# Finishing one tile ahead of the other in a layer's last down phase, and letting VectorE scale in the first K phase

## The chip, the cores and the metric

The kernel runs on one core of a Trainium2 chip. The metric is the device time of one execution in microseconds (us), lower is better. Most executions of one kernel lie within 0.2% of their median, some 2 us here.

## The reference, cut to what matters

Two identical layers act on 2048 tokens of 576 channels. Each has a linear attention and a gated unit without a nonlinearity; both layers share their weights.

```python
def _A_ref(x, wqkv, w_phi, wo):                      # 32 heads of 18
    ...
    phi_q = concatenate([softmax(pq), softmax(-pq)]) # the same for phi_k
    kv  = einsum("bhsf,bhsd->bhfd", phi_k, v)        # a sum over ALL tokens
    z   = einsum("bhsf->bhf", phi_k)
    num = einsum("bhqf,bhfd->bhqd", phi_q, kv)
    ...
def _B_ref(x, w_gate, w_up, w_down):                 # 576 -> 4608 -> 576
    return einsum("bsf,fd->bsd", einsum(x, w_gate) * einsum(x, w_up), w_down)

for layer in (1, 2):
    x = x + _A_ref(_layernorm(x), wqkv, w_phi, wo)
    x = x + _B_ref(_layernorm(x), w_gate, w_up, w_down)
```

The sum over all tokens is what makes a seam: layer 2 can attend only when the last tile of layer 1 has gone through its down projection, its normalisation and its K and V.

## The kernel before

Tokens are worked on in 16 tiles of 128, two tiles to a block, so each layer has eight blocks. A block has a gate/up phase and then a down phase. The engine programs are laid out on the host by a list scheduler: tasks yield groups of instructions, and the scheduler takes the group that it believes can start first, from the fixed durations that are written into each `Op`. What a task waits for in the schedule ("wait", "sig") is not a wait on the chip; it only fixes the order in which instructions are issued.

The down phase sums both tiles step by step (36 steps, 512 + 64 columns for each tile). The 64 column sums of both tiles share bank Z:

```python
def t_down(self, L, b, on_block_done):
    gots = yield ("acqn", ["pb"], 3)
    X, Y, Z = [g_[1] for g_ in gots]
    for f in range(NF):                              # NF = 36
        c, fi = divmod(f, CH)                        # CH = 2 steps to one load
        if fi == 0:
            yield ("wait", ("wd", L, b, c))
        ops = []
        for sl in range(2):                          # both tiles in every step
            ops.append(Op(... matmul(ps[:, X or Y, 0:512], lhsT, w[:, 0:512]) ...))
            ops.append(Op(... matmul(ps[:, Z, 64 * sl:64 * sl + 64], lhsT, w[:, 512:576]) ...))
        yield ("ops", "pe", ops)
        if fi == CH - 1:
            yield ("rel", "wd", slot)                # the ring slot is free for the next load
    yield ("go", s.t_bepi(L, b, X, Y, Z, on_block_done), 8, ...)

def t_bepi(self, L, b, X, Y, Z, on_block_done):      # one task: tile 0's adds, then tile 1's
    ...
    for sl in range(2):
        yield ("ops", "dve", [add of 512 columns, add of 64 columns])
        yield ("sig", ("x2t", L, st_))
```

The down weights come through a ring of six slots (five `wdr` and one `wdx`), one load of 288 KB for two steps; 18 loads make a phase. The scaling of the normalisation is offered to several engines; `boot` is the first K phase, `fast` the two tiles at the seam:

```python
yield ("alt", [(eng, [Op(...)...])
       for eng, dur in (("pool", (800, 200)[:2 - fast]), ("dve", (400,)))[:1 + fast]]
       + ([("act", act)] if boot else []))
```

## Time and profile before

| what | value |
|---|---|
| time | 1115.49 us, median of 3 (1114.45 to 1117.24) |
| span of the profiled execution | 1113.9 us |
| TensorE busy | 1069.7 us, 96% of the span |
| K phase, until the first gate/up weight load (on the cut told under the result) | 117.6 us |
| last down phase of layer 1 to layer 2's first gate/up | 53.3 us |
| start of the last down phase to the end | 21.9 us |

A profile is read here from coarse to fine. The busy row and the 40 slices show which engine is full and where it is not. Where it is not, a chain or a timeline shows what it waits for; in a timeline line the columns are start, duration, engine, source line, operation, output and inputs, shapes, and in brackets the idle time before and what ended it. The lines themselves are in the prediction below.

### The profile page before, as it was taken

The page shows a single profiled execution, that of the slowest core. Times are in us where ns is not written, and L with a number is a line of the kernel's source. Part 1 is how long each engine was busy: PE and PEld are TensorE (multiplying, and loading weights), DVE is VectorE, ACT ScalarE, POOL GpSimd, SP SyncE. Part 2 cuts the span into 40 slices and gives each one's busy share as a digit, 9 for nine tenths or more (in the row PEclk, how much of TensorE's full clock was granted, in tenths as well). Part 3 has the DMA queues.
Part 4 walks back from the last instruction along what each step waited for, and adds up shares of the span by engine and source line. Part 5 has one row for each costly group of instructions (what it writes and reads, how often), then busy time and mean ns, then how long its engine had stood idle before and what let it go on. Part 6 is the DMA issues. An engine that isn't in the chain of part 4 may idle for free.

```text
span 1113.9 us, 33734 instructions
## 1 busy us (share of the span) xinstructions
PE 1069.7 (96%) x15280; PEld 835.1 (75%) x15342; DVE 588.4 (53%) x1184; ACT 374.4 (34%) x862; POOL 313.3 (28%) x334
## 2 busy tenths in 40 slices
PE   5788999999999999999999899999999999999998
PEld 4565886868687786869687678696969696969685
DVE  7788744647375564646453675444535353524231
ACT  7786631414133241414232463131313030402120
POOL 4885512424152432413220252121212030300000
PEclk9899999999999999999999999999999999999999
DMA  8494227273542616371523313717272726362604
GB/s 175 114 314 157 32 47 197 47 204 47 151 97 79 158 39 186 47 204 26 152 75 98 96 24 47 214 36 215 35 215 35 205 46 191 58 180 49 179 26 139
DMA packets 185002, 129.07 MB, mean 116 GB/s; under 512 B 103322, under 2 KB 183706, under 8 KB 183706
## 3 DMA queue, kind: packets, MB, share of 16 engines
q1 hardware_dynamic: 184858, 126.91, 44.4%
q8 instruction: 120, 1.97, 0.7%
q14 instruction: 24, 0.20, 0.0%
HBM read 100.75 MB, written 2.36 MB: 93 GB/s over the span
## 4 chain that ended last, share of the span: by engine, by line
PE 83%; DVE 7%; ACT 4%; DMA 3%; POOL 2%; issue 1%; SPq 0%; DVEq 0%; POOLq 0%; ACTq 0%
PE ps L1427 47%; PE ps L1497 20%; PE ps L1001 6%; PE ps L1500 4%; PE ps L989 3%; PE ps L1288 2%; DMA wdr<-in_B_w_down_dram 1%; PE ps L1169 1%; DVE ss L1116 1%; DVE dd L1048 1%; POOL dd L1127 1%; ACT hT L1473 1%; DVE mxmn L1034 1%; DVE hT L1475 1%; DVE mxmn L1029 1%
## 5 line engine op out<-in xcount | busy, mean ns | idle before, releaser
L1427 PE MATMUL ps<-xT,Wu 64*128 64x256 bf16 x4608 | 582.2, 269 | 0.0
L1427 PE MATMUL ps<-xT,Wg 64*128 64x256 bf16 x4608 | 579.8, 269 | 0.8 <-ACT xT L971 0.8
L1427 PEld LDWEIGHTS ps<-xT,Wu 64*128 64x128 bf16 x4608 | 431.8, 94 | 22.4 <-DVE hT L1475 1.6
L1427 PEld LDWEIGHTS ps<-xT,Wg 64*128 64x128 bf16 x4608 | 427.2, 94 | 27.0 <-issue 3.3
L1473 ACT CAST hT<-ps 128x512 bf16<-128x512 f32 x288 | 168.0, 583 | 567.8 <-PE ps L1427 526.6
L1475 DVE TENSOR_TENSOR hT<-ps,hT 128x512 bf16<-128x512 f32 x288 | 196.9, 689 | 216.1 <-ACT hT L1473 215.3
L1497 PE MATMUL ps<-wdr,hT 128*128 128x512 bf16 x913 | 237.3, 380 | 0.9 <-DMA wdr<-in_B_w_down_dram 0.9
L1427 PE MATMUL ps<-xT,Wr 64*128 64x256 bf16 x1152 | 190.0, 269 | 0.0
L1500 PE MATMUL ps<-wdr,hT 128*128 128x64 bf16 x960 | 185.0, 193 | 3.1 <-DMA wdr<-in_B_w_down_dram 0.4
L1497 PEld LDWEIGHTS ps<-wdr,hT 128*128 128x128 bf16 x960 | 93.8, 98 | 110.8 <-DMA wdr<-in_B_w_down_dram 2.5
L1127 POOL TENSOR_TENSOR dd<-dd,ss 128x576 bf16<-128x576 bf16 x119 | 136.8, 1172 | 124.9 <-ACT ss L1123 121.0
L1098 POOL TENSOR_TENSOR dd<-xT,mxq 128x576 bf16<-128x576 bf16 x56 | 63.9, 1163 | 320.6 <-DVE mxq L1094 320.6
L1522 DVE TENSOR_TENSOR x_sb<-ps,x_sb 128x512 bf16<-128x512 f32 x32 | 22.0, 687 | 225.6 <-PE ps L1500 225.6
L961 POOL TENSOR_SCALAR xln<-x_sb,nmean,rstd 128x576 bf16<-128x576 bf16 x104 | 62.5, 607 | 172.9 <-ACT rstd L950 108.8
L1116 DVE TENSOR_REDUCE ss<-dd 128x64 f32<-128x1152 bf16 x61 | 82.1, 1347 | 31.6 <-ACT dd L1110 31.5
L1500 PEld LDWEIGHTS ps<-wdr,hT 128*128 128x128 bf16 x960 | 94.3, 98 | 0.0
L1427 PEld LDWEIGHTS ps<-xT,Wr 64*128 64x128 bf16 x1152 | 82.8, 94 | 5.2
L1108 ACT ACTIVATE dd<-dd 128x576 bf16<-128x576 bf16 x61 | 41.7, 684 | 47.6 <-DVE dd L1048 30.9
L1039 POOL TENSOR_TENSOR dd<-psb,mxmn 128x576 bf16<-128x576 bf16 x26 | 30.2, 1163 | 80.6 <-DVE mxmn L1029 80.6
L1497 PE MATMUL ps<-wdx,hT 128*128 128x512 bf16 x177 | 50.8, 380 | 0.0
L933 DVE BATCH_NORM_STATS2 st<-x_sb 128x6 f32<-128x288 bf16 x120 | 46.0, 446 | 2.8 <-DMA x_sb<-in_A_x_dram 2.7
L1001 PE MATMUL ps<-Wo,oT 64*128 64x288 bf16 x504 | 44.0, 283 | 0.8
(123 smaller groups left out, 968.9 us busy)
## 6 DMA issues: line engine op xcount, KB each, us to landing
wdr<-in_B_w_down_dram SPq DMA_DIRECT2D x240, 288.0 KB, 3.5
wdx<-in_B_w_down_dram SPq DMA_DIRECT2D x48, 288.0 KB, 3.4
Wg<-in_B_w_gate_dram SPq DMA_DIRECT2D x4, 1152.0 KB, 16.4
Wu<-in_B_w_up_dram SPq DMA_DIRECT2D x4, 1152.0 KB, 18.5
x_sb<-in_A_x_dram SPq DMA_DIRECT2D x8, 288.0 KB, 3.1
out_dram<-x_sb SPq DMA_DIRECT2D x16, 144.0 KB, 2.3
Wraw<-in_A_wqkv_dram SPq DMA_DIRECT2D x8, 144.0 KB, 2.8
xT<-xln SPq DMA_TRANSPOSE x58, 2.6
```

What stands on the lines that cost most here:

```text
L933: ops.append(Op(d_dve(288), (lambda e, j=j, h=h, src=src: e.bn_stats(st[:, sl[j], 6 * h:6 * h + 6], src)), reads=rd, writes=[("st", sl[j], ...
L961: em = [(lambda e, j=j, a=a, b=b, c=c: e.tensor_scalar(xln[:, sl[j], a:b], x_sb[:, ss[j], c:c + b - a], s.nmean[:, sl[j]:sl[j] + 1], rstd[ ...
L1001: out.append(Op(61, (lambda e, h=h, k=k, st=(i == 0 and k == 0), sp=(i == 1 and k == 3): e.matmul(s.ps[:, banks[h], 0:N], L[r, k, :], Wm[r ...
L1098: yield ("ops", "pool", [Op(1150, (lambda e, d=d, mb=mb: e.tensor_tensor(d, p3, mb, ALU.subtract)), reads=[("xT", st_), ("mq", mq, br)], w ...
L1108: yield ("ops", "act", [Op(590, (lambda e: e.activation(de2, de2, ACTF.Exp, scale=-1.0)), reads=s.ddk(sm, 1), writes=s.ddk(sm, 1))])
L1116: Op(1320, (lambda e: e.tensor_reduce(ss[:, sm, :].rearrange("p (b g) -> p b g", b=2), e4, AX.X, ALU.add)), reads=s.ddk(sm, 0) + s.ddk(sm, ...
L1127: yield ("alt", [(eng, [Op(dur, (lambda e, ev=ev, rb=rb: e.tensor_tensor(ev, ev, rb, ALU.mult)), reads=s.ddk(sm, br) + [("ss", sm)], write ...
L1427: out.append(Op(54.3, (lambda e, bank=bank, cs=cs, lhsT=lhsT, rhs=rhs, st=st, sp=sp: e.matmul(ps[:, bank, cs].rearrange("p (a n) -> p a n" ...
L1473: yield ("ops", "act", [Op(540, (lambda e, gb=gb, p=p: e.copy(hT[:, p, :], ps[:, gb, :])), reads=[("gu", gb)], writes=[("hT", p)] + (s.raw ...
L1475: yield ("ops", "dve", [Op(625, (lambda e, ub=ub, p=p: e.tensor_tensor(hT[:, p, :], ps[:, ub, :], hT[:, p, :], ALU.mult)), reads=[("gu", u ...
L1497: ops.append(Op(d_pe(512), (lambda e, lhsT=lhsT, bank=bank, slot=slot, fi=fi, f=f: e.matmul(ps[:, bank, 0:512], lhsT, s.wslot(slot)[:, fi, ...
L1500: ops.append(Op(d_pe(64) + 3, (lambda e, lhsT=lhsT, sl=sl, slot=slot, fi=fi, f=f: e.matmul(ps[:, Z, 64 * sl:64 * sl + 64], lhsT, s.wslot(s ...
```

## The change

The intent has two parts. In the last down phase of each layer, TensorE finishes the first tile's sums three ring slots (six steps) ahead of the second's, so that tile 0's sum can be added and normalised (layer 1) or stored (layer 2) while tile 1 is still being summed. For that the phase takes a fourth bank, so tile 0's 64 columns can be read alone. And in the first K phase VectorE joins GpSimd and ScalarE as an engine that may scale a tile. Two details apply to all sixteen down phases: in the last step the 64 column matmul is issued before the 512 column one, and the adds of the two tiles are two tasks, each of which takes its 64 columns first.

```diff
--- before.py
+++ after.py
@@ -565,6 +565,7 @@
         self.pqp = (5, 5)
         self.pqg = 12
         self.NPQ = 2
+        self.NLAST = 3
         self.pqd = 100
         self.pqn = (16, 16)
         self.qcrit = False
@@ -961,7 +962,7 @@
             em = [(lambda e, j=j, a=a, b=b, c=c: e.tensor_scalar(xln[:, sl[j], a:b], x_sb[:, ss[j], c:c + b - a], s.nmean[:, sl[j]:sl[j] + 1], rstd[:, sl[j]:sl[j] + 1],
                                                                  ALU.add, ALU.mult)) for a, b, c in ((0, 576, 0), (576, 640, 512))[:2 - fast]]
             yield ("alt", [(eng, [Op(d, em[i], reads=[("x", ss[j], 0), ("x", ss[j], 1), ("nmean", sl[j]), ("rstd", sl[j])], writes=[("xln", sl[j])]) for i, d in enumerate(dur)])
-                           for eng, dur in (("pool", (800, 200)[:2 - fast]), ("dve", (400,)))[:1 + fast]] + ([("act", act)] if boot else []))
+                           for eng, dur in (("pool", (800, 200)[:2 - fast]), ("dve", (400,) if fast else (400, 200)))[:1 + (fast or boot)]] + ([("act", act)] if boot else []))
         for j in js:
             if fast:
                 (_, bank), = yield ("acqn", ["pb"], 1)
@@ -1481,52 +1482,74 @@
 
     def t_down(self, L, b, on_block_done):
         s = self
-        ps, hT = s.ps, s.hT
-        gots = yield ("acqn", ["pb"], 3)
-        X, Y, Z = [g_[1] for g_ in gots]
-        for f in range(NF):
+        hT = s.hT
+
+        last = b == NB - 1
+        NR = NF - CH * s.NLAST * last
+        gots = yield ("acqn", ["pb"], 3 + last)
+        X, Y, Z = [g_[1] for g_ in gots][0:3]
+        ZZ = (Z, gots[3][1]) if last else (Z, Z)
+
+        def mm(f, sl):
+            c, fi = divmod(f, CH)
+            slot = s.wd_slot[(L, b, c)]
+            bank = X if sl == 0 else Y
+            z = ZZ[sl]
+            c0 = 256 * (f % 2) + 128 * sl
+            lhsT = hT[:, f // 2, c0:c0 + 128]
+            rd = [("hT", f // 2), ("wdr", slot)]
+            ops = [Op(d_pe(512), (lambda e: e.matmul(s.ps[:, bank, 0:512], lhsT, s.wslot(slot)[:, fi, 0:512], start=(f == 0), stop=(f == NF - 1))),
+                      reads=rd, writes=[("acc", bank)], excl=[("pb", bank)]),
+                   Op(d_pe(64) + 3, (lambda e: e.matmul(s.ps[:, z, 64 * sl:64 * sl + 64], lhsT, s.wslot(slot)[:, fi, 512:576],
+                                                        start=(f == 0 and (sl == 0 or last)), stop=(f == NF - 1), skip_group_check=True)),
+                      reads=rd, writes=[("acc", z)], excl=[("pb", z)])]
+            return ops[::-1] if f == NF - 1 else ops
+
+        for f in range(NR):
             c, fi = divmod(f, CH)
             if fi == 0:
                 yield ("wait", ("wd", L, b, c))
-            slot = s.wd_slot[(L, b, c)]
-            ops = []
-            for sl in range(2):
-                bank = X if sl == 0 else Y
-                c0 = 256 * (f % 2) + 128 * sl
-                lhsT = hT[:, f // 2, c0:c0 + 128]
-                ops.append(Op(d_pe(512), (lambda e, lhsT=lhsT, bank=bank, slot=slot, fi=fi, f=f: e.matmul(
-                    ps[:, bank, 0:512], lhsT, s.wslot(slot)[:, fi, 0:512], start=(f == 0), stop=(f == NF - 1))),
-                    reads=[("hT", f // 2), ("wdr", slot)], writes=[("acc", bank)], excl=[("pb", bank)]))
-                ops.append(Op(d_pe(64) + 3, (lambda e, lhsT=lhsT, sl=sl, slot=slot, fi=fi, f=f: e.matmul(
-                    ps[:, Z, 64 * sl:64 * sl + 64], lhsT, s.wslot(slot)[:, fi, 512:576],
-                    start=(f == 0 and sl == 0), stop=(f == NF - 1), skip_group_check=True)),
-                    reads=[("hT", f // 2), ("wdr", slot)], writes=[("acc", Z)], excl=[("pb", Z)]))
-            yield ("ops", "pe", ops)
+            yield ("ops", "pe", mm(f, 0) + mm(f, 1))
             if fi == CH - 1:
-                yield ("rel", "wd", slot)
+                yield ("rel", "wd", s.wd_slot[(L, b, c)])
+        for sl in range(2):
+            for f in range(NR, NF):
+                c, fi = divmod(f, CH)
+                if fi == 0:
+                    yield ("wait", ("wd", L, b, c))
+                yield ("ops", "pe", mm(f, sl))
+                if sl == 1 and fi == CH - 1:
+                    yield ("rel", "wd", s.wd_slot[(L, b, c)])
+            if sl == 0 and last:
+                for nxt, prio, name in on_block_done(L, b):
+                    yield ("go", nxt, prio, name)
+                yield ("go", s.t_bepi(L, b, 0, X, ZZ[0], True), 11, "bepi%d" % b)
         s.dn_active = False
         yield ("sig", ("dn", L, b))
-        yield ("go", s.t_bepi(L, b, X, Y, Z, on_block_done), 8, "bepi%d" % b)
-
-    def t_bepi(self, L, b, X, Y, Z, on_block_done):
-        s = self
-        ps, x_sb = s.ps, s.x_sb
-        for nxt, prio, name in on_block_done(L, b):
-            yield ("go", nxt, prio, name)
-        for sl in range(2):
-            st_ = 2 * b + sl
-            bank = X if sl == 0 else Y
-            xa = x_sb[:, st_, 0:512]
-            xb = x_sb[:, st_, 512:576]
-            yield ("ops", "dve", [
-                Op(d_dve(512), (lambda e, xa=xa, bank=bank: e.tensor_tensor(xa, ps[:, bank, 0:512], xa, ALU.add)),
-                   reads=[("acc", bank), ("x", st_, 0)], writes=[("x", st_, 0)], excl=[("pb", bank)]),
-                Op(d_dve(64), (lambda e, xb=xb, sl=sl: e.tensor_tensor(xb, ps[:, Z, 64 * sl:64 * sl + 64], xb, ALU.add)),
-                   reads=[("acc", Z), ("x", st_, 1)], writes=[("x", st_, 1)], excl=[("pb", Z)])])
-            yield ("rel", "pb", bank)
-            yield ("sig", ("x2t", L, st_))
-        yield ("rel", "pb", Z)
-        yield ("sig", ("x2", L, b))
+        if not last:
+            for nxt, prio, name in on_block_done(L, b):
+                yield ("go", nxt, prio, name)
+            yield ("go", s.t_bepi(L, b, 0, X, Z, False), 8, "bepi%d" % b)
+        yield ("go", s.t_bepi(L, b, 1, Y, ZZ[1], True), 11 if last else 8, "bepi%d" % b)
+
+    def t_bepi(self, L, b, sl, bank, z, free):
+        s = self
+        st_ = 2 * b + sl
+        if sl == 1:
+            yield ("wait", ("x2t", L, st_ - 1))
+        xa = s.x_sb[:, st_, 0:512]
+        xb = s.x_sb[:, st_, 512:576]
+        ops = [Op(d_dve(512), (lambda e: e.tensor_tensor(xa, s.ps[:, bank, 0:512], xa, ALU.add)),
+                  reads=[("acc", bank), ("x", st_, 0)], writes=[("x", st_, 0)], excl=[("pb", bank)]),
+               Op(d_dve(64), (lambda e: e.tensor_tensor(xb, s.ps[:, z, 64 * sl:64 * sl + 64], xb, ALU.add)),
+                  reads=[("acc", z), ("x", st_, 1)], writes=[("x", st_, 1)], excl=[("pb", z)])]
+        yield ("ops", "dve", ops[::-1])
+        yield ("rel", "pb", bank)
+        if free:
+            yield ("rel", "pb", z)
+        yield ("sig", ("x2t", L, st_))
+        if sl == 1:
+            yield ("sig", ("x2", L, b))
 
     def t_store(self, b):
         s = self
```

## The prediction

> **What bounds the kernel now.** I read the page first (busy shares and the 40 slices), then the chain that ended last in order of time, then the timeline and the busy table of the places that the change touches. The page says that this is a TensorE kernel with two soft spots:
>
> ```profile
> PE 1069.7 (96%) x15280; PEld 835.1 (75%) x15342; DVE 588.4 (53%) x1184; ACT 374.4 (34%) x862; POOL 313.3 (28%) x334
> ...
> PE   5788999999999999999999899999999999999998
> ```
>
> TensorE is busy in nine tenths of every slice but the first four (a slice is 27.8 us), slice 23 and the last one. The first four are the first K phase (layer 1 normalises, projects K and V and sums its state); slice 23 is the seam in which layer 1's last block has to be summed, normalised and turned into K before layer 2 can start. Between them run the sixteen gate/up and down phases, where TensorE is full: nothing that the change does can shorten those. The change removes no matmul, so only the three places where TensorE waits can pay: **the K phase, the seam, the end.** The table of these stretches (busy time of each engine):
>
> ```profile
> core 0: us, PE busy (x) PEld busy (x) DVE busy (x) ACT busy (x) POOL busy (x), PEclk, DMA share, GB/s
> 12.00:101.00 89.00, 68.24 (x562) 49.04 (x560) 78.34 (x160) 67.53 (x182) 65.38 (x65) 0.88 0.67 190
> ...
> 618.90:653.30 34.40, 28.97 (x268) 22.29 (x266) 26.60 (x59) 20.06 (x52) 9.58 (x8) 1.00 0.08 25
> ```
>
> In the K phase VectorE is the busiest engine, 78.34 of 89 us, with GpSimd at 65.38. In the seam TensorE fills itself with Q projections, but the chain through it is VectorE and ScalarE work on the last two tiles. Its start, in VectorE's timeline:
>
> ```profile
> 618.88 0.69 DVE L1522 TENSOR_TENSOR x_sb<-ps,x_sb 128x512 bf16<-128x512 f32 x1 [15.67 <-PE ps L1500]
> 619.49 0.22 DVE L1524 TENSOR_TENSOR x_sb<-ps,x_sb 128x64 bf16<-128x64 f32 x1
> 619.74 0.82 DVE L933 BATCH_NORM_STATS2 st<-x_sb 128x6 f32<-128x288 bf16 x2
> ...
> 621.40 0.43 DVE L961 TENSOR_SCALAR xln<-x_sb,nmean,rstd 128x576 bf16<-128x576 bf16 x1 [0.41 <-ACT rstd L950]
> 621.75 0.68 DVE L1522 TENSOR_TENSOR x_sb<-ps,x_sb 128x512 bf16<-128x512 f32 x1
> ```
>
> Tile 0's sum starts at 618.88, just when the down phase ends. Tile 1's sum is ready at the same moment but is taken at 621.75, after tile 0's whole normalisation. So the two tiles are ready together and are then served one after the other; an earlier tile 0 moves the queue. The end shows the same pair:
>
> ```profile
> 1109.58 0.69 DVE L1522 TENSOR_TENSOR x_sb<-ps,x_sb 128x512 bf16<-128x512 f32 x1 [16.13 <-PE ps L1500]
> 1110.19 0.21 DVE L1524 TENSOR_TENSOR x_sb<-ps,x_sb 128x64 bf16<-128x64 f32 x1
> 1110.32 0.68 DVE L1522 TENSOR_TENSOR x_sb<-ps,x_sb 128x512 bf16<-128x512 f32 x1
> 1110.43 1.09 SPq L1535 DMA_DIRECT2D out_dram<-x_sb  x2
> 1110.92 0.21 DVE L1524 TENSOR_TENSOR x_sb<-ps,x_sb 128x64 bf16<-128x64 f32 x1
> ```
>
> Two tiles' adds follow the last matmul serially, then the second store lands (2.3 us, median of the page's DMA table); the span is over at 1113.9.
>
> **What the Trainium skill says.** "PSUM — Partial Sum Buffer", section "PSUM bank collisions raise a hardware error": two engines must not be in one bank at once, so accesses are guarded by bank, not by address. That is why the change takes a fourth bank in the last phase: the 64 leftover columns of both tiles share bank Z now, and tile 0's could not be read while tile 1's are still being summed. No run here shows a collision; the kernel orders accesses by bank. "SBUF — State Buffer", section "Who interferes with whom": a VectorE instruction with two SBUF inputs, or one in a two-port mode such as tensor_scalar can enter, shuts GpSimd out for its whole length. The trace agrees as to the first kind: the GpSimd multiply that starts at 635.89, beside a VectorE multiply of 0.76 us, takes 1.73 us, where the group's mean is 1172 ns. "VectorE: DVE Perf Modes", section "The perf-mode tier table", lets tensor_scalar on bf16 run at four elements a cycle; the trace has 429 ns for 576 elements (mean of 6), which is 1.34 elements a ns, well short of that rate, so I use 429.
>
> **The change, part by part.**
>
> (1) *Order of the last down phase.* A down step is 512 + 64 columns for each tile. In the timeline one tile's pair starts every 0.245 us (1094.71, 1094.95, 1095.20). Three ring slots are 6 steps, so tile 0 runs its last 6 pairs in 6 x 0.245 = 1.47 us, then tile 1 its 6 in another 1.47 us. TensorE's total is unchanged; tile 0's sum is ready 5 to 6 pairs earlier than now, about 1.4 us, if the weights are there.
>
> (2) *Are the weights there?* Two tiles drain a slot in 0.98 us, one tile alone in 0.49. Tile 0 thus wants the next-to-last slot 0.49 us and the last slot 0.98 us earlier than today. At the seam the next-to-last slot is late already:
>
> ```profile
> 611.89 5.05 DMA wdr<-in_B_w_down_dram
> 616.94 0.05 issue
> 616.98 0.39 PE ps L1497
> ```
>
> (The chain: the load issued at 611.89 lands at 616.94; TensorE waits 0.23 us.) The same load would now be wanted at 616.75 - 0.49 = 616.26, so TensorE waits about 0.7 us instead of 0.2, and runs tile 0's last two slots from 616.98 to about 617.96. Tile 0 is ready there instead of at about 618.7: **0.7 us earlier, half of the ideal.** Tile 1 then ends 6 x 0.245 later, 619.4, against 618.9 now; but it isn't wanted before tile 0's normalisation has left VectorE. At the end of the kernel the loads took 2.9 to 4.3 us (median 3.6) and nothing waited: the last one, issued at 1103.97, should land near 1107.6, and tile 0 would want it at about 1107.9. I count no stall there.
>
> (3) *Seam.* VectorE's queue there starts 0.7 us sooner, and tile 1's add, now behind tile 0's scaling, moves with it: 618.88 to 621.75 is 2.87 us of VectorE sequence, so tile 1 would be taken at about 618.05 + 2.87 = 620.9, well after its sum is there (619.4). From 621.4 to 637.6 the chain alternates between VectorE, ScalarE, TensorE's 1.4 us projections and a GpSimd multiply, without slack that I could name, so the 0.7 us should reach the start of layer 2's gate/up at 653.29. Taking the 64 columns first (they wait for a matmul that ends before the 512 one) may add 0.1. **Seam: -0.8 us.**
>
> (4) *End.* Tile 0's two adds (0.8 us) and its store now lie under tile 1's matmuls. After the last matmul, whose end stays near 1109.8, only tile 1's 512 add (0.68) is left, so it is done at 1110.5 instead of 1111.13 (1110.92 + 0.21). **End: -0.6 us.**
>
> (5) *Scaling on VectorE in the first K phase.* Of the 16 tiles GpSimd scales 10 now (820 + 393 ns each, 1.21 us with both parts) and ScalarE 6 (866 + 245 ns, and a 0.29 us product before it, 1.40 us). VectorE would need 429 ns for 576 columns and, estimated from its small instructions (0.15 to 0.26 us for 64 columns or fewer), 0.2 for the rest: 0.63 us. What it can relieve:
>
> ```profile
> 17.84 2.60 POOL L961 TENSOR_SCALAR xln<-x_sb,nmean,rstd 128x576 bf16<-128x576 bf16 x4 [1.04 <-ACT rstd L950]
> ...
> 25.00 1.39 POOL L853 TENSOR_TENSOR BDphi<-wst,mask 128x720 bf16<-128x720 bf16 x1 [3.44 <-DMA wst<-in_A_w_phi_dram]
> ...
> 27.49 1.31 POOL L961 TENSOR_SCALAR xln<-x_sb,nmean,rstd 128x576 bf16<-128x576 bf16 x2
> ...
> 29.91 1.31 POOL L961 TENSOR_SCALAR xln<-x_sb,nmean,rstd 128x576 bf16<-128x576 bf16 x2
> ```
>
> The chain of the first 35 us runs along these GpSimd lines. The two tiles at 17.84 sit ahead of a wait for the phi weights (3.44 us), which would absorb what is saved there. The two at 27.49 and 29.91 had their rstd from ScalarE long before and only queue behind that wait; on VectorE they would be done two to three us sooner and GpSimd's multiplies, which release TensorE's sums at 32.40, would come 2.6 us sooner. Against this, VectorE is full from 10 to 32 us (10.00 of 10.00 in 20 to 30) and then idles for 1.92 us before 34.21 and 2.23 before 37.79. The schedule is laid out on the host by a greedy list scheduler that gives each tile to the engine it believes free first, with VectorE's cost weighted by 1.2; I guess that 4 to 7 tiles move, 2.5 to 4.4 us more on the busiest engine, most of it paid out of those idle stretches. From 83 to 101 us VectorE works without a gap, so what is gained early is passed on only if its backlog there also starts earlier. I choose **-1.2 us**, with a spread of some 2.5 either way, because a different order of issue reshuffles the whole phase.
>
> (6) *A fourth bank.* At the last down phase of layer 2 six banks belong to gate/up, whose first pair is free by then, and two to nobody: four are there, no wait. In layer 1 the state sums of layer 2 (from 599.70) take one bank at a time with a higher priority, so the phase may start a little later or have its order against them changed: +0.2 us, a guess within the 1.7 us that these sums take.
>
> Sum: -0.8 - 0.6 - 1.2 + 0.2 = -2.4 us, so 1115.49 - 2.4 = **1113.1 us.**
>
> **The rivals.** *The weights eat it all*: if the last two loads at the seam come later still (the largest landing time there is 5.0 us), tile 0 gains nothing and TensorE ends 1 us later, so seam and fourth bank together cost about +0.5: total near 1114.0. For it speaks the wait that is already there; against it that only one of 16 down phases matters. *VectorE becomes the bound of the K phase*: with 78 of 89 us busy, 6 tiles x 0.63 = 3.8 us more could lengthen the phase by up to that: 1117. For it the gapless stretch from 83 us on; against it some 10 us of idle VectorE earlier, where the scaling lies. *GpSimd's chain was the bound*: four tiles fewer take 4 x 1.21 = 4.8 us off it, and all of it arrives: near 1109.5. *Nothing but the end survives*, because the scheduler puts the scaling where it would have waited anyway: 1114.9.
>
> **Range and chances.** The two sure pieces are small (1.4 us together); the K phase sets the spread. I give 1109.0 to 1116.5, which covers all but the worst of the rivals. Two per cent would be 22.3 us; the whole of TensorE's idle time in the span is 1113.9 - 1069.7 = 44 us, and only some 15 us of it lie where the change acts. Chances: faster by over 2% 0.02, within 2% 0.96, slower 0.02.
>
> **What would show it.** In the changed trace: the first of the two last 512 adds should begin over 1 us before the last matmul, and the end of the last add should follow that matmul by about 0.7 us; at the seam, tile 0's add at 0.7 us before its present place relative to the start of that down phase, with a wait for a wdr load of about 0.7 us in TensorE's list; the time from tile 0's add to layer 2's first gate/up unchanged at 34.4 us; 4 to 7 tiles of scaling on VectorE before 60 us, and the first gate/up (now 117.85) starting 1.2 us sooner. I am wrong if the K phase moves by more than 3 us either way, if a new wait for a bank shows at the start of the last down phase, or if the gate/up and down phases in between change length by more than 1 us, which I take as fixed.

## The result, and the profile after

| | before | after |
|---|---|---|
| median, us | 1114.97 (1113.39 to 1117.24, 4 runs) | 1111.77 (1111.19 to 1112.81, 4 runs) |
| span of the profiled execution, us | 1113.9 | 1109.5 |

The ratio is 0.9971, with a 95% interval of 0.9951 to 0.999: 3.2 us faster. A ratio here is the mean time of one kernel's fast runs over that of the other's from the same rounds, so it is not quite the ratio of the medians. The predicted 1113.1 us is 1.3 us too high, inside its range. The rest of this document asks whether it was right for its reasons.

The page of the changed kernel, busy row and slices of TensorE. The first slice gained a tenth and the fourth lost one; the rest of the gain is too small for this view:

```profile
PE 1072.4 (97%) x15342; PEld 832.2 (75%) x15342; DVE 586.1 (53%) x1192; ACT 373.7 (34%) x855; POOL 311.4 (28%) x330
...
PE   6787999999999999999999899999999999999998
```

To see where the time went I cut every profiled execution at the starts of its gate/up and down phases, from the weight load records of the trace. These cuts lie 0.1 to 0.2 us before those of the profile's own times and are compared only among themselves. "Seam" is from the start of layer 1's last down phase to layer 2's first gate/up; "middle" from layer 1's second gate/up phase to that down phase; "layer 2" from its first down phase to its last. All in us, one execution each:

| program | first gate/up | middle | seam | seam and the phase after | layer 2 | end |
|---|---|---|---|---|---|---|
| before | 117.64 | 417.77 | 53.25 | 95.50 | 396.46 | 21.93 |
| before, again | 117.05 | 418.34 | 52.84 | 95.09 | 394.97 | 21.94 |
| after | 116.51 | 416.54 | 52.96 | 95.21 | 394.90 | 21.68 |
| after, again | 117.09 | 416.98 | 52.48 | 94.73 | 395.79 | 21.54 |

Between the first profiles of each, the differences are -1.13 (K phase), -1.23 (middle), -0.29 (seam), -1.56 (layer 2) and -0.25 (end), which make up the 4.4 us between the two spans. Layer 2 is the largest, and it is chance: the second profile of the kernel before has 394.97 there too. With two executions of each the sum is -0.55 - 1.30 - 0.33 - 0.37 - 0.33 = -2.9 us, near the 3.2 of the times. **The middle, which I had called fixed, gives as much as any place that the change was made for.**

The seam in VectorE's timeline, after. Tile 0's adds come first, as planned; then, between tile 0's statistics and its scaling, the adds of tile 1:

```profile
615.93 0.23 DVE L1544 TENSOR_TENSOR x_sb<-ps,x_sb 128x64 bf16<-128x64 f32 x1 [15.07 <-PE ps L1503]
616.13 0.69 DVE L1542 TENSOR_TENSOR x_sb<-ps,x_sb 128x512 bf16<-128x512 f32 x1
...
618.03 0.21 DVE L1544 TENSOR_TENSOR x_sb<-ps,x_sb 128x64 bf16<-128x64 f32 x1
618.16 0.68 DVE L1542 TENSOR_TENSOR x_sb<-ps,x_sb 128x512 bf16<-128x512 f32 x1
618.76 0.42 DVE L962 TENSOR_SCALAR xln<-x_sb,nmean,rstd 128x576 bf16<-128x576 bf16 x1
```

In the kernel before, tile 1's adds followed the scaling. The chain that ended last shows what held tile 0's sum: a weight load issued at 610.51 that lands 4.88 us later, for which the waits view counts 0.8 us of TensorE (0.7 was predicted):

```profile
610.51 4.88 DMA wdx<-in_B_w_down_dram
615.43 0.39 PE ps L1501
```

The end. Tile 0 is added under tile 1's matmuls, the last of which ends at 1105.93; the last add ends 0.73 us after it:

```profile
1104.29 0.23 DVE L1544 TENSOR_TENSOR x_sb<-ps,x_sb 128x64 bf16<-128x64 f32 x1 [15.06 <-PE ps L1503]
1104.50 0.69 DVE L1542 TENSOR_TENSOR x_sb<-ps,x_sb 128x512 bf16<-128x512 f32 x1
1105.76 0.23 DVE L1544 TENSOR_TENSOR x_sb<-ps,x_sb 128x64 bf16<-128x64 f32 x1 [0.57 <-PE ps L1503]
1105.97 0.69 DVE L1542 TENSOR_TENSOR x_sb<-ps,x_sb 128x512 bf16<-128x512 f32 x1
```

The K phase, busy times from 12 to 101 us (columns as in the prediction), and two of the five tiles that VectorE scales now:

```profile
12.00:101.00 89.00, 69.23 (x572) 48.72 (x573) 83.67 (x169) 65.19 (x178) 65.83 (x64) 0.96 0.68 190
```

```profile
28.84 1.16 DVE L962 TENSOR_SCALAR xln<-x_sb,nmean,rstd 128x576 bf16<-128x576 bf16 x2 [0.56 <-ACT rstd L951]
...
57.84 1.68 DVE L962 TENSOR_SCALAR xln<-x_sb,nmean,rstd 128x576 bf16<-128x576 bf16 x2
```

VectorE's busy time in this window grew from 78.34 to 83.67 us. It scales five tiles now, two that were GpSimd's and three that were ScalarE's, and a pair of scalings takes 1.05 to 1.64 us of busy time (the lines run from the first start to the last end) where I had estimated 0.63. The two lines of the K phase differ in one thing more: the granted clock of TensorE (the third figure from the end) is 0.88 before and 0.96 after; run 2 comes back to this.

### The profile page after: what moved, and what is told of

The parts are those of the page before. It is cut to its first block, busy times and chain, and to the rows that moved or that the text cites. A ratio compares the mean times of both kernels' runs of the same rounds, so it can differ in the third digit from the quotient of the medians.

```text
span 1109.5 us, 33782 instructions
## 1 busy us (share of the span) xinstructions
PE 1072.4 (97%) x15342; PEld 832.2 (75%) x15342; DVE 586.1 (53%) x1192; ACT 373.7 (34%) x855; POOL 311.4 (28%) x330
## 4 chain that ended last, share of the span: by engine, by line
PE 87%; DVE 4%; DMA 1%; ACT 1%; POOL 1%; issue 0%
PE ps L1428 50%; PE ps L1501 22%; PE ps L1002 7%; PE ps L1503 3%; PE ps L990 2%; PE ps L1289 2%; PE ps L1170 1%; DVE ss L1117 1%; POOL dd L1128 1%; DVE x_sb L1364 1%; DMA oT<-dd 1%; DMA wdr<-in_B_w_down_dram 0%; DMA wdx<-in_B_w_down_dram 0%; DVE mxmn L1035 0%; DVE dd L1049 0%
## 5 line engine op out<-in xcount | busy, mean ns | idle before, releaser
L1501 PE MATMUL ps<-wdr,hT 128*128 128x512 bf16 x960 | 245.2, 380 | 1.0 <-DMA wdr<-in_B_w_down_dram 1.0
L1428 PE MATMUL ps<-xT,Wr 64*128 64x256 bf16 x1152 | 184.9, 269 | 0.0
L1544 DVE TENSOR_TENSOR x_sb<-ps,x_sb 128x64 bf16<-128x64 f32 x32 | 7.0, 220 | 228.6 <-PE ps L1503 228.6
L1428 PEld LDWEIGHTS ps<-xT,Wr 64*128 64x128 bf16 x1152 | 78.1, 94 | 5.2
L1501 PE MATMUL ps<-wdx,hT 128*128 128x512 bf16 x192 | 54.3, 380 | 0.1
```

The costliest lines, as they stand in the source:

```text
L1428: out.append(Op(54.3, (lambda e, bank=bank, cs=cs, lhsT=lhsT, rhs=rhs, st=st, sp=sp: e.matmul(ps[:, bank, cs].rearrange("p (a n) -> p a n" ...
L1501: ops = [Op(d_pe(512), (lambda e: e.matmul(s.ps[:, bank, 0:512], lhsT, s.wslot(slot)[:, fi, 0:512], start=(f == 0), stop=(f == NF - 1))), ...
```

## The experiments

Twelve runs were made, five rounds each: ten new kernels and each of the two unaltered ones once more. With intervals of about 0.15% the times alone cannot tell 1.5 us from nothing. All results were correct by the comparison with the reference. The first four runs split the change into its parts.

**1. The kernel before again** (no edit).

> The kernel before, profiled a second time, to see what differs between two executions of one program. Theory: the down phases of layer 2 that were longer in the first profile (19.06, 18.78 us against 18.18) are waits for weight loads that come and go, so another profile has them elsewhere or not at all; the gate/up phases repeat within 0.1 us; the first gate/up starts within 0.5 us of 117.6 us unless the half-clock windows fall otherwise. Ratio of the times 1.000, within 0.0015. Rival: the long down phases belong to the program, then they repeat at the same places.

Measured: 1114.66 us, ratio 0.9995 [0.9982, 1.0007]; stretches as in the table above. Layer 2 took 394.97 us where the first profile had 396.46, so the 1.5 us that the two first profiles differ there is no effect of the change. The first gate/up came 0.59 us sooner, a little more than the expected 0.5, with a granted clock of 0.96 from 12 to 101 us where the first profile had 0.88. The loads that were waited for in the first profile, from its chain, are absent in the second:

```profile
703.28 5.52 DMA wdr<-in_B_w_down_dram
874.30 5.25 DMA wdx<-in_B_w_down_dram
```

**2. Only the VectorE scaling.**

```diff
-  ("dve", (400,)))[:1 + fast]]
+  ("dve", (400,) if fast else (400, 200)))[:1 + (fast or boot)]]
```

> Only the scaling on VectorE in the first K phase is added to the kernel before. Theory: it brings the first gate/up from 117.6 to about 116.5 us and nothing else: pairs of down and gate/up phases of layer 1 stay at 62.56 us, the seam (start of the last down phase to layer 2's gate/up) at 53.25, the end at 22.0. Time -1.1 us, ratio 0.999. Rival: the 1.1 us were only the luck of where the half-clock windows of TensorE fell in the first profile (0.88 against 0.96 mean clock from 12 to 101 us); then the first gate/up starts at 117.6 here whenever the windows fall as before.

Measured: 1114.13 us, ratio 0.9988 [0.9975, 1.0]. The first gate/up starts at 116.80 us; middle 417.98, seam 52.84 and end 21.99 us are those of the kernel before, and layer 2 had late loads (397.65). One execution is not enough for the K phase, since the first matmul, which waits for the raw K and Q weights, alone started between 5.1 and 5.6 us. Over all fourteen profiles, the five of kernels without this edit start gate/up at 116.69 to 118.00 us, mean 117.45, and the nine with it at 115.52 to 117.09, mean 116.22: **-1.2 us.** The rival named above, the granted clock, is not excluded by these means: from 12 to 101 us it was 0.88 to 0.96 in the five (mean 0.91) and 0.90 to 0.98 in the nine (mean 0.95). Compared at one clock, there are few: at 0.90 the one without the edit starts gate/up at 116.69 and the two with it at 117.09 and 116.80; at 0.96 the one without at 117.05 and the four with it at 115.71 to 116.74 (mean 116.26). So the nine are faster, but how much of the 1.2 us is the scaling and how much the clock stays open.

**3. Only the order of the down phases** (everything but the VectorE scaling).

> Only the new order of the last down phase with its split epilogue, without VectorE in the K phase. Theory: first gate/up at 117.6 as before; the pairs of phases in layer 1 at 62.28 instead of 62.56, because TensorE's order there is the one of the changed kernel (fewer interruptions); seam 52.95 against 53.25; end 0.2 to 0.6 us shorter than 22.0, by the wait for a weight load. Time -1.7 us, ratio 0.9985. Rival: the pairs shortened because of the other K phase; then they are 62.56 here and 62.28 in the run with the scaling alone.

Measured: 1113.07 us, ratio 0.9982 [0.9969, 0.9994]. First gate/up 116.69 (117.6 was expected; the clock is part of run 2's open question), middle 416.36, seam 52.21, layer 2 396.09, end 22.14 us. The middle is 1.4 to 2.0 us shorter than in the two profiles of the kernel before, so its gain belongs to this half of the change. The end did not gain: its last down phase waited 0.8 us for a weight load.

**4. The same without the head start** (in the program of 3, zero slots ahead instead of three; fourth bank, swap and split adds stay).

```diff
-        self.NLAST = 3
+        self.NLAST = 0
```

> As the run with the order alone, but with no ring slot run ahead: both tiles end together, the fourth bank and the two adds as tasks of their own stay. Theory: the middle phases still 62.28, as TensorE's order there is that of the changed kernel; no wait for the last weight loads beyond the 0.2 us of before; tile 0's sum starts 0.5 us later relative to the phase than with three slots, seam about 53.2; end 22.0. Time -1.2 us, ratio 0.999. Rival: running ahead is what pays; then seam and end are each 0.5 us or more worse than in the run with the order alone.

Measured: 1114.58 us, ratio 0.9991 [0.9978, 1.0005]. Middle 416.56, seam 54.24, seam and the phase after 95.52, end 22.17 us. The middle is short although nothing runs ahead. The seam is longer than before: with the adds in two tasks tile 1's come 0.8 us after tile 0's (18.58 and 19.39 us after the phase's start) and ahead of tile 0's statistics. (The scheduler also moved a Q projection into the seam here, out of a phase that became 1 us shorter; hence the column for both.) So the split of the adds by itself gains nothing at the seam (95.52 against 95.50 and 95.09 before); the head start has to pay.

**5. The swap alone.** Runs 3 and 4 left two edits that reach every down phase: the swap of the last step's matmuls, and the adds in two tasks. Building each alone and comparing the order of TensorE's instructions showed that only the swap changes it. So the kernel before was run with this edit:

```diff
-            yield ("ops", "pe", ops)
+            yield ("ops", "pe", [ops[1], ops[0], ops[3], ops[2]] if f == NF - 1 else ops)
```

> The kernel before with one edit: in the last step of each down phase the 64 column matmul goes before the 512 column one. Nothing else of the change is in it. Theory (this swap alone moves TensorE's order in the middle of layer 1, through the list scheduler, and that is the 1.5 us that I had not predicted): from the start of the second down phase to the start of the sixteenth 416.3 to 416.7 us instead of 417.8 to 418.3; the waits of the weight loads of gate/up for hT of the kernel before (about 1.4 us, five of them) are gone; the K phase, the seam (53 us from the last down phase of layer 1 to layer 2's first gate/up) and the end (22.0 us) are as before; ratio to the kernel before about 0.9987. Rival (the 1.5 us come from the split of the two tiles' adds into tasks of their own): middle 417.8 to 418.3, ratio 1.000.

Measured: 1114.8 us, ratio 0.9977 [0.9962, 0.9993]; middle **416.78 us**, first gate/up 117.88, seam 53.05, end 21.96 us. The middle is shorter and all else is as before. What the swap does to the order of TensorE in a period of the middle (runs of instructions of one kind in program order; gu is gate/up, kv the state sums, num the numerators):

```
before: gu92 Wo10 gu20 Wo8 gu104 Wo10 gu20 Wo8 gu144 Wk10 gu20 Wk8 gu88 Wv10 gu16 Wv8 gu40 Wk10 gu16 Wk8 gu56
        Wv10 gu16 Wv8 gu16 num12 down16 num12 down4 kv6 down8 kv8 down4 kv6 down112
swap:   gu92 Wo10 gu20 Wo8 gu72 Wo10 gu16 Wo8 gu108 Wk10 gu20 Wk8 gu104 Wv10 gu20 Wv8 gu20 Wk10 gu16 Wk8 gu72
        Wv10 gu16 Wv8 gu72 num12 kv6 down8 kv8 num12 down8 kv6 down128
```

The matmuls are the same, and the phases are interleaved differently: the second V projection ends 72 gate/up matmuls before the down phase instead of 16. In the waits of TensorE's weight loads between 182 and 540 us (columns: line, what for, us in total, times, longest), the kernel before had

```profile
PEld ps L1427 <- DVE hT L1475: 1.4, 5, 0.3
```

one for each of the five regular periods, 0.28 us each; a period (down and gate/up) takes 62.56 us in it and 62.28 with the swap. This line is gone with the swap.

**6. The changed kernel without the swap** (the undo of 5).

```diff
-            return ops[::-1] if f == NF - 1 else ops
+            return ops
```

> The changed kernel with the swap of the two matmuls of the last step undone; split last phase, fourth bank, VectorE scaling and split adds stay. Theory: the middle of layer 1 is back at 417.8 to 418.3 us, so this kernel is 1.5 us slower than the changed one (ratio to before about 0.9985 where the changed kernel had 0.9971). Seam and end as in the changed kernel within 0.3 us. Rival: middle stays at 416.5 and only seam and end lose 0.1 each.

Measured: 1115.36 us, ratio 0.999 [0.9978, 1.0003]; middle 419.54, first gate/up 116.09, seam 52.56, end 22.06 us. The same wait is back, five times:

```profile
PEld ps L1428 <- DVE hT L1476: 1.4, 5, 0.3
```

The middle is even 1.2 us above the higher one of the kernel before; late transposes (1.4 us of waits for them, 0.4 before) go with that. Without the swap most of the change's gain is lost. Over all profiles the four without the swap have a middle of 417.77 to 419.54 us (mean 418.41), the ten with it 416.01 to 417.82 (mean 416.83): **-1.6 us.** The order of TensorE's weight loads in the middle, read from the traces, is one and the same in those four and another, again the same, in those ten, so no other edit touches it. The end, too, lost 0.4 us, most of it to a longer wait for loads (its last down phase takes 18.08 us against 17.84 and 17.71 in the changed kernel).

**7. Tile 0 scaled before tile 1 is added.** The task of tile 1's adds waits, in the schedule, until tile 0's scaling is laid out.

```diff
+        yield ("sig", ("scaled", sig[0]))          # after the scaling
 ...
+            if L == 1 and b == NB - 1:             # before tile 1's adds
+                yield ("wait", ("scaled", ("xTk", 0)))
```

> The changed kernel, but at the seam tile 1's two adds are held back in the schedule until tile 0's scaling has been laid out. Theory (the change lost half of its gain at the seam because tile 1's adds went ahead of tile 0's scaling on VectorE): tile 0's scaling follows its statistics without the 0.3 to 0.6 us of tile 1's adds; layer 2's first gate/up comes about 0.3 us sooner after the start of the last down phase of layer 1; as the scheduler moves one Q projection from the seam into the first gate/up phase, the sum of seam and that phase (95.2 us in the changed kernel) is what counts, and it should be about 94.9. Rival (the chain has another limit behind it, so the order of these adds is free): 95.2 or more.

Measured: 1113.96 us, ratio 0.9977 [0.9964, 0.9989]; seam 52.17, the phase after it 43.35 instead of 42.25, the two together 95.52 us. The order is as wanted:

```profile
617.86 0.43 DVE L962 TENSOR_SCALAR xln<-x_sb,nmean,rstd 128x576 bf16<-128x576 bf16 x1 [0.41 <-ACT rstd L951]
618.20 0.22 DVE L1547 TENSOR_TENSOR x_sb<-ps,x_sb 128x64 bf16<-128x64 f32 x1
618.34 0.68 DVE L1545 TENSOR_TENSOR x_sb<-ps,x_sb 128x512 bf16<-128x512 f32 x1
```

Tile 0's scaling starts 2.59 us after its first add instead of 2.83, and the first gate/up comes 34.49 us after that add instead of 34.71, so tile 1's adds did cost 0.2 to 0.25 us. But the scheduler moved one Q projection out of the seam, where TensorE had time for it, into a gate/up phase, where it has none, and that costs 1.1 us. The expected 94.9 was missed: as a version this edit loses 0.3 us.

**8. Half of the bytes in the last loads.** Loads 6 to 17 of the last down phase of each layer carry half of their bytes. This was meant to give a wrong result; the comparison passed all the same, so stale weights in one block of eight stay within its tolerance, and the pass says nothing here. The compute engines have the same instructions in the same order.

```diff
- e.dma_start(s.wslot(slot), wdv[:, CH * c:CH * c + CH, :])
+ e.dma_start(s.wslot(slot)[:, 0:h, :], wdv[:, CH * c:CH * c + h, :])   # h = 1 if last block and c >= 6 else CH
```

> Wrong result on purpose: the changed kernel with the same instructions in the same order on the compute engines, but the last 12 weight loads of the last down phase of each layer carry half of their bytes. Theory (tile 0 runs into the weights because it drains a slot in half of the time): the waits of the down phase for wdr loads at the seam (0.8 us) and at the end (0.33 us) go, the first of the last 512 adds comes 1.3 to 1.5 us before the second at both places, seam 52.2 to 52.5 us instead of 52.96, end 21.5 us instead of 21.85. Rival (these waits are chance of one execution or have another cause than the bytes): both unchanged.

Measured: 1111.35 us, ratio 0.9961 [0.9946, 0.9976]; seam **51.75**, seam and the phase after 94.00, end 21.33 us. Tile 0's first add at the seam, in this trace whose phase starts at 597.45 by the profile's own times:

```profile
614.48 0.23 DVE L1544 TENSOR_TENSOR x_sb<-ps,x_sb 128x64 bf16<-128x64 f32 x1 [13.86 <-PE ps L1503]
```

It comes 17.03 us after the start of its phase, against 18.25 and 17.77 in the changed kernel and 18.84 and 18.43 before. So at the seam weight loads took 0.7 to 1.2 us of what the head start could give, more than I had expected of this run, and at the end 0.2 to 0.35 us. The waits for weights are gone in both places.

**9. The changed kernel again** (no edit; sent together with 10 and 11).

> The changed kernel unaltered, to see how far its stretches repeat beside the others of this call. Expected: first gate/up at 115.7 to 116.8 us, the middle of layer 1 416.4 to 417.2, seam 52.6 to 53.1, end 21.6 to 21.9, layer 2 between 394.9 and 397.7; ratio 0.997 to 0.998.

Measured: 1112.46 us, ratio 0.9977 [0.9959, 0.9995]; stretches as in the table above, within what was expected but for the first gate/up (117.09), the seam (52.48) and the end (21.54), each just outside.

**10. Five slots ahead instead of three.**

```diff
-        self.NLAST = 3
+        self.NLAST = 5
```

> The changed kernel with five ring slots instead of three by which tile 0 runs ahead. Theory (weights set when tile 0 is done): tile 0 wants the last slot another 0.98 us sooner, which no load can give, so its sum comes no sooner (first 512 add at the seam 18.3 to 18.6 us after the start of that down phase) while tile 1 ends about 1 us later: in the last down phase the wait for loads grows from 0.3 to about 1.3 us and the end becomes 22.5 to 22.8 us instead of 21.7; seam plus first gate/up phase 95.2 to 95.6 us. Rival (the split's own size sets the gain): tile 0 comes 0.9 us sooner, seam 52.0, end unchanged at 21.7.

Measured: 1114.86 us, ratio **1.0** [0.9985, 1.0016]: the whole gain of the change is gone. At the seam tile 0's first add comes 17.68 us after the phase's start, no sooner than in the second profile of the changed kernel (17.77), and the sum of seam and the phase after is 96.19 us. In the waits of TensorE there:

```profile
PE ps L1501 <- DMA wdr<-in_B_w_down_dram: 1.4, 1, 1.4
```

The waits are not the whole of it: as in run 7 the scheduler moved one Q projection out of the seam, and the phase after it takes 43.35 us instead of 42.25. So 1.1 us of that sum goes with this move, and the seam alone (52.84) lies between the two of the changed kernel (52.48 and 52.96). At the end the wait is 0.5 us and the end 22.21 us, less than the expected 22.5 to 22.8, because tile 0 came 0.3 to 0.45 us sooner there after all. The middle was 417.82 and the layer 2 stretch 395.88 us in this execution, which this edit does not touch; so the ratio overstates the loss, of which some 1.2 us at the seam and 0.6 us at the end can be seen.

**11. A ring of eleven slots in layer 2.** The K and V weights are dead once layer 2 has its last K and V. Five more slots are laid over them:

```diff
+        self.wdy = AT("wdy", [128, 5, CH, D], BF16, addr(self.Wk))     # Wk and Wv lie side by side
+    def t_grow2(self):
+        for st_ in range(NS):
+            yield ("wait", ("ain", 2, st_))
+        for i in range(5):
+            yield ("rel", "wd", s.NWD + 1 + i, 0.0)
```

> The changed kernel, and in layer 2 the ring of down weights has 11 slots instead of 6: the five new ones lie in the K and V weights, which are dead by then. TensorE's order stays the same instruction for instruction. Theory (the spread of layer 2's down phases, 18.18 to 19.3 us, and the wait of 0.3 us in the last one are loads of down weights that come late by chance): every down phase of layer 2 at 18.18 us, or 17.51 for the last two; from layer 2's second phase to the start of the last down phase 394.5 to 395 us where other executions had 394.9 to 397.7; the end 21.3 to 21.4 us instead of 21.68; seam unchanged. Ratio to before about 0.9955. Rival (the spread comes from something else, gate/up's own waits or the clock): the spread stays and only the end gains 0.3.

Measured: 1110.14 us (1109.44 to 1111.33), ratio **0.9959** [0.9944, 0.9974], the lowest; the changed kernel beside it had 1112.46. TensorE's program is the same. Every down phase of layer 2 takes 18.18 us (17.51 the last two) and the layer 2 stretch 394.90 us. Of twelve executions with the six slot ring ten had at least one longer down phase in layer 2, on average 0.98 us of excess in an execution. The end did not gain as expected: the last add is 0.2 to 0.33 us sooner, but the kernel ends 3.09 us after it instead of 2.80. The trace shows the queue's closing waits one after the other, 0.06 us apart, and the ring brought five more of them (0.30 us).

**12. One more slot at the seam too.** In addition to 11, the last load of layer 1's last down phase goes into two tiles of xT that are dead there, so it can start with the phase.

```diff
+        self.wdz = AT("wdz", [128, CH, D], BF16, addr(self.xT) + 1280 * (NS - 2))
+        yield ("dma", ..., e.dma_start(s.wdz[:], wdv[:, NF - CH:NF, :]), writes wdz, xT 14, xT 15)
```

> The changed kernel with both: the 11 slot ring in layer 2, and for the last down phase of layer 1 one more slot for its last load, in the two tiles of xT that are dead from the last gate/up matmul of layer 1 until the seam writes them again. That load starts with the phase instead of 11.8 us into it, and each of the other eleven has one chunk of time (0.98 us) more. TensorE's order is the same. Theory (load stalls took 1.2 us from tile 0 at the seam, as the half loads showed): the waits for weights in that phase fall from 0.6 to 1.4 us to at most 0.3, tile 0's first add comes 17.1 to 17.4 us after the phase's start (17.8 to 18.3 in the changed kernel), seam 51.8 to 52.1 us instead of 52.5 to 53.0; layer 2 again without spread (394.9); ratio to before about 0.9950 where the 11 slots alone had 0.9959. Rival (the loads share one limit of bytes, so a load more at the start delays those behind it): tile 0 no sooner than 17.8.

Measured: 1110.53 us, ratio 0.9963 [0.995, 0.9977]; seam 53.04 us, tile 0's first add 18.33 us after the phase's start. That is the rival's number: no gain. TensorE waits as long as before, for the load ahead of the new one, which takes 5.46 us; and the DMA busy row (tenths in 40 slices, 594 to 616 us) is nearly full from the seventeenth slice on:

```profile
PE ps L1532 <- DMA wdr<-in_B_w_down_dram: 1.1, 1, 1.1
```

```profile
DMA  0010049479149579998999999799999879998500
```

Twelve loads of 288 KB want to pass in the phase, and an earlier start of one did not help the others. Run 8 shows that the bytes matter; that the full DMA engines are the limit is what both suggest, and it is not shown apart from the order of the loads in their queue. What would bring fewer bytes into this phase, for instance weights that stay, was not tried.

The traces hold another candidate for the late loads, which no run above was made to test. In the changed kernel's window of this phase (597 to 620 us) the DMA view shows, beside the loads, one fetch of instructions:

```profile
q8 instruction: 1, 0.02, 0.3%
```

In all fourteen executions one such packet of 16 KB starts 13.0 to 15.2 us into layer 1's last down phase. It takes 0.88 to 1.30 us, where a packet of weights takes about 0.06 on the mean. In thirteen of the fourteen a load in flight there takes 0.6 to 2.3 us longer to land than the load before it; in run 12 it was the 2.3. Over all executions, of the 268 loads of down weights that took over 0.7 us longer than the one before, 205 (76%) were in flight together with an instruction fetch, against 34% of all loads. So the loads that seemed late by chance come mostly with these fetches. No run moved a fetch, so that the fetch makes them late is not shown; run 8 had one too, and its load took 3.72 us instead of 2.17 but, with half of the bytes, was still in time.

## Why the prediction was right or wrong, point by point

The total was right (1113.1 predicted, 1111.77 measured), but not by its own sum. Two of its terms came out at half or less, one agrees in the mean though its cause is not separated from the clock, one did not exist, and an effect that it excluded made up for the difference.

1. *"nothing that the change does can shorten those"* (the gate/up and down phases in between): **wrong, and the step that failed.** The prediction said it would be wrong if they changed by more than 1 us; they changed by 1.3 between the two profiles of each kernel, and by 1.6 over all fourteen. Runs 5 and 6 tie this to the swap of two matmuls, which I had counted at 0.1 us at the seam. The phases were not as full as one digit of a slice says: five waits of 0.28 us lay in the weight loads' own queue, and the host's scheduler, given another last step, laid out another order. That it came out shorter was luck of the order, not intent; no run explains why the scheduler chose it.
2. *K phase -1.2 us*: **right in size by the mean** over all profiles, -1.2, but the kernels with the edit also had the higher granted clock (0.95 against 0.91; run 2), so some of the agreement may be luck. Five tiles moved where I said 4 to 7, and only two of them came from GpSimd, on whose relief the argument rested. The price was wrong: a pair costs VectorE 1.22 us on average, not 0.63. The 576 column part took 415 to 774 ns, and the 64 column part, which I had put at 200, took 333 to 1225 ns; the long ones lay beside GpSimd's own work. That the phase did not become longer for it fits with the idle time of VectorE that the prediction named; no run shows that this was the reason.
3. *Seam -0.8 us*: **direction right, size wrong**, -0.3. The head start itself was sized well: tile 0's add came 0.6 us sooner against 0.7, with a wait for weights of 0.8 against 0.7. The step that failed is "tile 1's add, now behind tile 0's scaling, moves with it". The adds are a task of their own now, with the highest priority, and the scheduler put them ahead of the scaling; run 7 measures this at 0.2 to 0.25 us. From tile 0's add to layer 2's gate/up it takes 34.71 us, where I expected an unchanged 34.4.
4. *End -0.6 us*: **mechanism right**: the last add ends 0.73 us after the last matmul (0.7 predicted), and in runs 11 and 12, without late loads, the last add is 0.58 to 0.59 us sooner after the phase's start than in the kernel before. "I count no stall there" failed: loads cost 0.2 to 0.35 us in the changed kernel, and its end gained 0.3 in the two profiles of each kernel. Over the five executions with three slots ahead, six ring slots and full loads the end is 21.84 us on the mean, against 21.96 in the four with the old order: 0.1. What the head start gives there, late loads mostly take back.
5. *Fourth bank +0.2 us*: **not there.** The stretch before the last down phase of layer 1 is 40.50 us in both kernels, and no wait for a bank shows.
6. *The rivals.* "The weights eat it all" came true in part; in run 10 the gain was gone, but 1.1 us of that went with the moved Q projection. "VectorE becomes the bound" and "GpSimd's chain was the bound" did not: the K phase moved by 1.2 us, not by 4. Two figures here do not follow from the prediction's own numbers: with its other terms, 3.8 us more in the K phase make 1118.1, not 1117; and the idle time of TensorE where the change acts is 20.8 us in the K phase and 5.4 in the seam by its own table, not some 15.

Sum by the means over all profiles of one order: -1.2 (K phase) - 1.6 (middle) - 0.35 (seam, 52.64 in five against 53.00 in four) - 0.1 (end) = about -3.3 us, against -3.2 in the first comparison and -2.6 in the second (0.9977).

## What to carry to other kernels

When a program is laid out by a scheduler, no edit is local: compare the order of instructions on every engine before calling a phase fixed, and undo the small edits one at a time, since the smallest one may carry the gain. Running one tile ahead of another also asks for its inputs sooner; look at how late the last loads are today before choosing how far ahead, since with five slots instead of three tile 0 came no sooner at the seam, and TensorE's longest wait there was 1.4 us instead of 0.6 to 0.8. Before you call a load late by chance, look at what else the DMA engines carry at that time. And before you credit an edit with a gain in a phase in which the granted clock varies, compare executions at one clock. Memory that is dead in a later stage can make a prefetch ring longer at no cost in compute; this, and not a further turn of the change itself, gave the fastest version here.

## What the Trainium skill lacked or had wrong

- "VectorE: DVE Perf Modes", section "The perf-mode tier table", gives tensor_scalar on bf16 for one size (693 ns for 2048 elements, four per cycle). Its section on the trn2 errata lets other sizes be worked out, with a fixed term of about 150 cycles, so the cost of a small one isn't lacking, but it is not what the runs show: at 0.96 GHz and four per cycle an estimate from the page is 306 ns for 576 elements and 173 for 64. Measured on VectorE in the K phase were 415 to 473 ns for 576 in four of five cases, and 333 at best for 64, often beside GpSimd's scalings; without GpSimd beside them, 576 elements took 429 to 430 ns in the changed kernel.
- "SBUF — State Buffer", section "Who interferes with whom", says that whoever comes first holds the shared ports for the whole instruction. The runs agree in kind (a 64 column scaling took 1225 ns beside GpSimd's work, and GpSimd's own 820 ns grew to 1000), but no run here shows each delay as exactly one instruction of the other engine. The prediction left out the page's condition, who comes first.
- "DMA: Bandwidth & Descriptors", section "Bandwidth", times single transfers issued from GpSimd (0.95 us for 64 KB, 6.15 us for 1 MB). How long a load takes with several others in flight on SyncE's queue is lacking, and it matters here: 288 KB loads landed in a median of 3.4 to 3.8 us, and in 4.1 to 5.5 us where TensorE waited for them at the seam.
- No page that I found has what an instruction fetch costs the loads in flight: its 16 KB packet took 0.88 to 1.30 us at the seam, and 76% of the loads that were suddenly late were in flight with one.
- No page that I found has the cost of a wait on a semaphore that is already satisfied (the nearest is a time for reading one): on SyncE they follow each other 0.06 us apart, and five more of them at the end cost 0.3 us.
